# Chunks 16 to 31 of a chunked state-space attention: scores in four groups of 32 rows, scores and decay in the same four PSUM banks

## The chip, the core and the metric

The kernel runs on one core of a Trainium2 chip. The metric is the device time of one execution in microseconds, as the median of several runs. TensorE multiplies matrices into PSUM (eight banks of 512 fp32 values in each of 128 partitions), VectorE and ScalarE read PSUM and SBUF, GpSimd works on SBUF alone and issues DMAs, SyncE issues DMAs.

## The reference

Three layers follow one another: a chunked linear attention with decay (4 batches, 8 heads, 768 positions, head width 32, state width 16), a two-layer MoE with a leaky activation, and a gated two-layer MoE. Cut to what matters here:

```python
for c in range(nc):                         # chunks along the sequence
    cum = np.cumsum(la, axis=-1)
    L = np.exp(cum[:, :, :, None] - cum[:, :, None, :]) * causal
    CB = np.einsum('bhin,bhjn->bhij', Cc, Bc)
    y = np.einsum('bhij,bhjd->bhid', CB * L, xc)
    y += np.einsum('bhin,bhnd->bhid', Cc, state) * np.exp(cum)[..., None]
    state = decay_full * state + sum_j(Bc * xc * decay_from_j)
h = x @ w_in
x = (np.maximum(h, 0.0) + alpha * np.minimum(h, 0.0)) @ w_out
gate = 1.0 / (1.0 + np.exp(-(x @ w_gate)))
out = (gate * (x @ w_val)) @ w_out2
```

## The kernel before

The sequence is cut into chunks of T = 96 positions, eight for each batch, 32 in all. The state is carried as 16 further rows of the chunk, so W = 112 rows stand for 96 positions and 16 state entries. For one chunk c:

- `ev_decay(c)` multiplies a left tile `dl` with a right tile `dr` into the PSUM tile `d` (two banks, tag "d"), two matmuls of 384 columns, and ScalarE's exp turns that into `lt` (L337).
- `ev_scores(c)` computes C times B into the PSUM tile `cb` (two banks, tag "cb", L351). Each of its two matmuls uses 64 rows of the array: 4 heads of 16 state entries, with C laid out in blocks so that each head meets its own columns (4 x 96 = 384).
- `ev_weigh(c)` multiplies scores and decay on VectorE into `mt` (L358), and B with the last column of the decay into `bd` (L365; not in the last chunk of a batch).
- `ev_out(c)` runs `yd` = x times `mt` (L386), and x times `bd` for the next state (L380); ScalarE copies the state (L396) and the output (L398).

The first MoE layer is interleaved: from iteration `lead` = 7 on, each iteration i also does one step of it. `moe1_in` (L429) multiplies into the one-bank tile `h`, ScalarE makes `t` (L434), VectorE makes `g` from `h` and `t` (L436). In the next iteration `halves` splits `g` into `gh` (ScalarE, L449) and `gl` (VectorE, L450), and `moe1_out` (L473) accumulates into `acc`. When a run of such steps ends, `acc` is copied or added out (L485 to L488). Between them `feed(n, ...)` does n of the operations that unpack the MoE weights, on VectorE and ScalarE (L138 to L181); GpSimd fetches their raw words.

The schedule is manual: every engine does its instructions in the order in which the loop writes them. Iteration i writes, in turn: the product of scores and decay of chunk i, `halves` of the step before, the decay of chunk i + 1, some weight operations, the MoE step, the output of chunk i - 1, the scores of chunk i + 1, the MoE output of the step before, and more weight operations. Every tag in PSUM has one buffer here; a matmul into it waits until the readers of its last content are done. `load_cum`, `load_x` and `load_bc` issue the loads for chunk i + 3 on SyncE; B and C of four chunks (a group) come in five DMAs.

Of the kernel before, what the change touches and what calls it, by code (L numbers as in the profile page):

```python
# [18 lines left out]
T = 96  # L19
# [9 lines left out]
WG = 256  # L29

RAWS = 4

OPS = 7

# [13 lines left out]
def kernel(  # L48
# [46 lines left out]
    ring = ctx.enter_context(tc.tile_pool(name="ring", bufs=2))  # L95
    psum = ctx.enter_context(tc.tile_pool(name="psum", bufs=1, space=PSUM))
    dram = ctx.enter_context(tc.tile_pool(name="dram", bufs=1, space=DRAM))

    alpha_sb = cpool.tile([128, NF1], F32, name="alpha_sb")
    sign = cpool.tile([128, NF1], F32, name="sign")  # L100
# [117 lines left out]
    c0 = 4 * G * N + H  # L218
    misc = apool.tile([128, T + W], F32, name="misc")
    units_c = apool.tile([128, N], F32, name="units")  # L220
    mask_c = misc[0:T, 0:T]
    left_c = misc[0:T, T:T + W]
    eye_c = apool.tile([N, N], F32, name="eye")
# [26 lines left out]
    def load_x(c):  # L250
# [4 lines left out]
        if k == 0:  # L255
            nc.gpsimd.memset(t[T:W, 0:H * D], 0.0)

    def load_bc(c, e=None):


        if c < ND:
            BC[c] = aring.tile([128, W + 4 * T], F32, tag="bc0", name="bct", bufs=1)
            nc.sync.dma_start(out=BC[c], in_=bc0[:, c])
        else:
            g = c // G
            e = e or nc.sync
            e.dma_start(
                out=bt[g % NG][:, :, 0:T], in_=bc[g][:, 0].rearrange("p (g t) -> p g t", t=T)
            )
            src = bc[g][:, 1].rearrange("(m q) t -> q m t", q=NP)  # L270
# [39 lines left out]
            out=cum_d.rearrange("b h l s -> (b h l) s"), in_=bf(parts)  # L310
        )

    LT, MT, BD, CBT = {}, {}, {}, {}
    lead = -(-BL // T) + 1

    def ev_decay(c):

        d = psum.tile([W, 2, 512], F32, tag=("d", "acc")[c % 2] if c < lead else "d", name="d")
        for e in range(2):
            hs = slice(4 * e, 4 * e + 4)  # L320
            if c >= DIRECT:
                nc.tensor.matmul(  # L322
                    d[:, e, 0:4 * T], dl[c % NC], dr[c % NC][:, hs, :], start=True, stop=True
                )
                continue
            nc.tensor.matmul(
                d[:, e, 0:4 * T], early_l[:, c], early_r[:, hs, :],
                start=True, stop=False, skip_group_check=True,
            )
            for q in range(4):  # L330
                nc.tensor.matmul(
                    d[:, e, q * T:(q + 1) * T], early_i[:, 4 * e + q],
                    parts[0:2 * H, c * T:(c + 1) * T],
                    start=False, stop=True, skip_group_check=True,
                )
        LT[c] = t = aring.tile([W, H, T], F32, tag="lt", name="lt", bufs=2)
        nc.scalar.activation(  # L337
            t.rearrange("j (e h) t -> j e (h t)", e=2), d[:, :, 0:4 * T], AF.Exp
        )

    def ev_scores(c):

        cb = psum.tile([W, 2, 512], F32, tag="cb", name="cb")
        for e in range(2):
            r = slice(64 * e, 64 * e + 64)
            if c < ND:
                left, right = BC[c][r, 0:W], BC[c][r, W:]
            else:
                g, i = divmod(c, G)
                left, right = bt[g % NG][r, i], ct[g % NG][r, :, i * T:(i + 1) * T]  # L350
            nc.tensor.matmul(cb[:, e, 0:4 * T], left, right, start=True, stop=True)  # L351
        CBT[c] = cb

    def ev_weigh(c):
        MT[c] = m = aring.tile([W, H, T], F32, tag="mt", name="mt", bufs=2)

        split = "j (e q) t -> j e q t" if c < ND else "j (q e) t -> j e q t"
        nc.vector.tensor_tensor(  # L358
            m.rearrange(split, e=2),
            CBT.pop(c)[:, :, 0:4 * T].rearrange("j e (q t) -> j e q t", t=T),  # L360
            LT[c].rearrange(split, e=2), op=ALU.mult,
        )
        if c % CPB < CPB - 1:
            BD[c] = bd = aring.tile([W, H, N], F32, tag="bd", name="bd")
            nc.vector.tensor_tensor(  # L365
                bd, b_of(c), LT[c][:, :, T - 1:T].broadcast_to([W, H, N]), op=ALU.mult
            )

    def ev_out(c):

# [49 lines left out]
        nc.scalar.copy(t[:, 0], src)  # L420
        nc.vector.tensor_tensor(t[:, 1], src, bf(t[:, 0]), op=ALU.subtract)

    def moe1_in(k, f, tag):
        need(2 * (f // 2))
        h = psum.tile([128, BL], F32, tag=tag, name="h")
        w = win[f // 2][:, :, :, (f % 2) * 128:(f % 2 + 1) * 128]
        for i, (wl, xl) in enumerate(((1, 0), (0, 0), (0, 1))):
            for kt in range(KT):
                nc.tensor.matmul(  # L429
                    h, w[:, wl, kt, :], xh["m1", k][:, xl, kt, :],  # L430
                    start=(i == 0 and kt == 0), stop=(i == 2 and kt == KT - 1),
                )
        t = ring.tile([128, BL], F32, tag="s", name="t")
        nc.scalar.activation(t, h, AF.Identity, scale=sign[:, f:f + 1])  # L434
        g = ring.tile([128, BL], F32, tag="g", name="g")
        nc.vector.scalar_tensor_tensor(  # L436
            g, h, salpha[:, f:f + 1], t, op0=ALU.mult, op1=ALU.max
        )
        gt["m1", k, f] = g
# [23 lines left out]
    def moe1_out(k, f, two=True):  # L463
        need(2 * (f // 2) + 1)
        first, last = ends[k, f]
        if first:
            accs[0] += two
            acc[k] = psum.tile([128, KT, BL], F32, tag=("acc", "d")[accs[0] % 2], name="acc")
        gh, gl = gt.pop(("m1", k, f))
        w = wout[f // 2][:, :, f % 2, :]  # L470
        for i, (wl, g) in enumerate(((1, gh), (0, gh), (0, gl))):
            for m in range(KT):
                nc.tensor.matmul(  # L473
                    acc[k][:, m], w[:, wl, m * 128:(m + 1) * 128], g,
                    start=(first and i == 0), stop=(last and i == 2),
                )
        if last and two:
            moe1_done(k)
# [15 lines left out]
    def moe2_in(k, f, tag):  # L494
        need(first2 + 3 * (f // 2) + 1)
        gate = psum.tile([128, BL], F32, tag=tag, name="gate")
        if f % 2 == 0:
            vt[k] = psum.tile([128, 2, BL], F32, tag="cb", name="val")
# [15 lines left out]
    def moe2_out(k, f):  # L514
        need(first2 + 3 * (f // 2) + 2)
        if f == 0:
            po[k] = [psum.tile([128, 2, 512], F32, tag=t, name="po") for t in ("acc", "d")]
        o = po[k]
        ph, pl = gt.pop(("m2", k, f))
        w = w2["out", f // 2][:, :, f % 2, :]  # L520
# [138 lines left out]
    def moe2_pair(k, j, before):  # L659
# [6 lines left out]
        a = two(psum.tile([128, BL], F32, tag="h", name="pa"))  # L666
        b = two(psum.tile([128, BL], F32, tag="y", name="pb"))
        if j % 2 == 0:
            vt[k] = psum.tile([128, 2, BL], F32, tag="cb", name="pc")
# [75 lines left out]
    with tc.manual_schedule():  # L745
# [5 lines left out]
        def step_in(i, tag):  # L751
            kind, k, f = steps[i]
            (moe1_in if kind == "m1" else moe2_in)(k, f, tag)

        def step_out(i, **kw):
            kind, k, f = steps[i]
# [13 lines left out]
        def keep_busy(n):  # L770
            p = psum.tile([128, 512], F32, tag="h", name="nobody")
            for _ in range(n):
                nc.tensor.matmul(p, heat[:, 0:128], heat, start=True, stop=True)
# [31 lines left out]
            load_x(i)  # L805
        take_up()
        nc.gpsimd.dma_start(out=alpha_sb, in_=alpha)

        def setup_units(j):
            nc.gpsimd.tensor_scalar(  # L810
                bt[j][:, :, T:W], units_c.unsqueeze(1).broadcast_to([128, G, N]),
                2.0, None, op0=ALU.mult,
            )

        copy_eye(0)
        setup_units(0)
# [88 lines left out]
        at = 0  # L905
        for i in range(NCH + 1):
            go = i >= lead
            if i < NCH:
                ev_weigh(i)

            if i == lead // 2 + 1:
# [5 lines left out]
            if i == 1:  # L917
                setup_left(1)
                load_cum(4)
                scale(0)  # L920
                for j in range(2):
                    setup_right(j)
                keep_busy(2)
            if 1 <= i <= 3:
                follow(i)
                ahead[0] += i != 2
                take_up()
# [7 lines left out]
                halves(steps[at - 1])  # L935
            if at > 1 and ends[steps[at - 2][1:]][1]:
                moe1_done(steps[at - 2][1])
            if i + 1 < NCH:
                ev_decay(i + 1)
            now = 0 if i == 0 else EARLY if not go else FIRST if at < half else LATER  # L940
            feed(now // 2, first2)
            if go:
                step_in(at, "h")
            if i > 0:
                ev_out(i - 1)
            if i + 1 < NCH:
                ev_scores(i + 1)
            if not go:
                keep_busy(3 if i < 3 else 2)
# [9 lines left out]
            if i == -(-2 * BL // T):  # L959
                split_x("m1", 1)  # L960
        need(first2 - 1)
        actx.close()
        p2 = ctx.enter_context(tc.tile_pool(name="p2", bufs=1))

# [127 lines left out]
```

## Time and profile before

| | |
|---|---|
| median of 3 runs | 636.93 us (636.29 to 638.09) |
| the profiled execution's own time | 638.78 us |
| its span in the profile | 637.0 us |
| TensorE busy | 625.9 us, 98% of the span |
| VectorE busy | 520.4 us, 82% |
| ScalarE busy | 364.7 us, 57% |
| GpSimd busy | 39.4 us, 6% |
| chunks 16 to 31, from the decay of 16 to the end of the last step | 71.5 to 147.2 us |

The span runs from the first to the last instruction of the profile. The execution's own time is longer by what lies around it. A busy share is a mean over all stages.

### The profile page before, as it was taken

To read this page: it belongs to the slowest core of one execution; us is meant where nothing else is said; L and a number is where in the kernel's file an instruction comes from. 1 tells how busy PE (TensorE), PEld (TensorE's weight loads), DVE (VectorE), ACT (ScalarE), POOL (GpSimd) and SP (SyncE) were. 2 spreads that over 40 slices of the span, in tenths; PEclk is the share of its full clock that TensorE was granted. 3 is DMA by queue.
4 is the path that set the end of the run, shared out by engine and by line. 5 is a ranking of instruction groups with operands and counts; after the bars stand their busy time and mean duration, and the time that the engine had idled before them with its cause. 6 is when DMAs were issued, how large, how long until landed. Compare 5 with 4: busy or idle time off the path is not lost.

```text
span 637.0 us, 11146 instructions
## 1 busy us (share of the span) xinstructions
PE 625.9 (98%) x4336; PEld 519.1 (81%) x4336; DVE 520.4 (82%) x910; ACT 364.7 (57%) x729; POOL 39.4 (6%) x68
## 2 busy tenths in 40 slices
PE   8799999999999999999999999999999999999997
PEld 4356666667888888888888888999999999999996
DVE  7799988865888878777676988888888888888876
ACT  7788877865666666566555435534534534534443
POOL 9211001000000000000000000000000000000000
PEclk9899999999999999999999999999999999999999
DMA  6744334410221221220000000100100100100100
GB/s 189 223 143 157 113 117 123 132 44 2 67 66 34 66 67 34 66 66 1 1 1 1 1 1 1 34 1 2 34 1 1 35 1 2 34 1 2 34 1 33
DMA packets 19270, 30.69 MB, mean 48 GB/s; under 512 B 7330, under 2 KB 14658, under 8 KB 19218
## 3 DMA queue, kind: packets, MB, share of 16 engines
q0 software_dynamic: 5232, 18.44, 9.2%
q1 hardware_dynamic: 13474, 11.08, 6.1%
q8 instruction: 34, 0.56, 0.4%
q10 hardware_dynamic: 512, 0.47, 0.2%
q14 instruction: 18, 0.15, 0.1%
HBM read 26.57 MB, written 3.34 MB: 47 GB/s over the span
## 4 chain that ended last, share of the span: by engine, by line
PE 92%; ACT 3%; DVE 2%; DMA 1%; issue 1%; POOL 0%; ACTq 0%; DVEq 0%
PE acc L473 21%; PE h L429 20%; PE pb L610 10%; PE po L552 10%; PE pa L610 7%; PE pc L610 7%; PE po L557 5%; PE cb L351 3%; PE gate L504 3%; PE val L504 3%; PE yd L386 1%; PE d L322 1%; DMA raw<-in_moe_w_in_dram 1%; PE yd L380 1%; ACT lt L337 1%
## 5 line engine op out<-in xcount | busy, mean ns | idle before, releaser
L429 PE MATMUL h<-xh,win 128*128 128x512 f32 x576 | 146.9, 390 | 0.5 <-ACT xh L420 0.5
L429 PEld LDWEIGHTS h<-xh,win 128*128 128x128 f32 x576 | 107.7, 188 | 22.3 <-ACT xh L420 0.8
L473 PE MATMUL acc<-gh,wout 128*128 128x512 f32 x384 | 105.8, 397 | 0.6 <-ACT x L398 0.6
L436 DVE SCALAR_TENSOR_TENSOR g<-h,salpha,t 128x512 f32<-128x512 f32 x96 | 71.9, 749 | 41.5 <-ACT t L434 41.2
L473 PEld LDWEIGHTS acc<-gh,wout 128*128 128x128 f32 x384 | 70.1, 188 | 27.0 <-ACT t L434 10.6
L434 ACT ACTIVATE t<-h,sign 128x512 f32<-128x512 f32 x96 | 66.0, 688 | 43.7 <-PE h L429 43.2
L449 ACT CAST gh<-g 128x512 fp32r<-128x512 f32 x96 | 59.7, 621 | 43.0 <-DVE g L436 43.0
L450 DVE TENSOR_TENSOR gl<-g,gh 128x512 fp32r<-128x512 f32 x96 | 66.0, 688 | 15.9 <-ACT gh L449 14.8
L719 ACT ACTIVATE s<-cs 128x512 f32<-128x512 f32 x30 | 19.0, 633 | 92.5 <-DVE cs L718 92.5
L552 PE MATMUL po<-w2out,gh 128*128 128x512 f32 x240 | 65.3, 394 | 0.0
L450 DVE TENSOR_TENSOR gl<-p,gh 128x512 fp32r<-128x512 f32 (+1 forms) x74 | 49.7, 672 | 12.6 <-ACT gh L449 12.6
L473 PE MATMUL acc<-gl,wout 128*128 128x512 f32 x192 | 59.2, 389 | 0.0
L449 ACT CAST gh<-p 128x512 fp32r<-128x512 f32 (+1 forms) x74 | 45.0, 610 | 20.8 <-DVE p L725 12.0
L552 PEld LDWEIGHTS po<-w2out,gh 128*128 128x128 f32 x240 | 41.8, 189 | 6.1
L610 PE MATMUL pa<-xh,w2in 128*128 128x256 f32 x300 | 44.0, 282 | 0.0
L473 PEld LDWEIGHTS acc<-gl,wout 128*128 128x128 f32 x192 | 36.0, 188 | 7.8
L557 PEld LDWEIGHTS po<-w2out,gl 128*128 128x128 f32 x240 | 36.3, 188 | 5.5 <-DVE gl L450 0.9
L610 PEld LDWEIGHTS pa<-xh,w2in 128*128 128x128 f32 x300 | 39.3, 190 | 0.0
L557 PE MATMUL po<-w2out,gl 128*128 128x256 f32 x240 | 38.0, 280 | 0.0
L337 ACT ACTIVATE lt<-d 112x768 f32<-112x768 f32 x32 | 26.0, 812 | 13.2 <-PE d L322 12.2
L694 DVE TENSOR_TENSOR cs<-pb,cs 128x512 f32<-128x512 f32 x30 | 20.7, 689 | 14.3 <-PE pb L610 14.3
L358 DVE TENSOR_TENSOR mt<-cb,lt 112x768 f32<-112x768 f32 x32 | 30.4, 949 | 0.2 <-ACT lt L337 0.2
(165 smaller groups left out, 1040.1 us busy)
## 6 DMA issues: line engine op xcount, KB each, us to landing
raw<-in_moe_w_out_dram POOLq DMA_DIRECT2D x14, 512.0 KB, 4.1
xs<-in_xb_dram SPq DMA_DIRECT2D x32, 144.0 KB
raw<-in_moe_w_in_dram POOLq DMA_DIRECT2D x8, 512.0 KB, 4.3
raw<-in_moe_w_gate_dram POOLq DMA_DIRECT2D x6, 512.0 KB, 4.1
raw<-in_moe_w_val_dram POOLq DMA_DIRECT2D x6, 512.0 KB, 4.1
out_dram<-osb SPq DMA_DIRECT2D x10, 256.0 KB
bt<-in_bc_dram SPq DMA_DIRECT2D x7, 192.0 KB
ct<-in_bc_dram SPq DMA_DIRECT2D x28, 48.0 KB
```

Source lines behind the costliest of these rows:

```text
L337: nc.scalar.activation(t.rearrange("j (e h) t -> j e (h t)", e=2), d[:, :, 0:4 * T], AF.Exp)
L358: nc.vector.tensor_tensor(m.rearrange(split, e=2), CBT.pop(c)[:, :, 0:4 * T].rearrange("j e (q t) -> j e q t", t=T), LT[c].rearrange(split ...
L429: nc.tensor.matmul(h, w[:, wl, kt, :], xh["m1", k][:, xl, kt, :], start=(i == 0 and kt == 0), stop=(i == 2 and kt == KT - 1),)
L434: nc.scalar.activation(t, h, AF.Identity, scale=sign[:, f:f + 1])
L436: nc.vector.scalar_tensor_tensor(g, h, salpha[:, f:f + 1], t, op0=ALU.mult, op1=ALU.max)
L449: nc.scalar.copy(gh[:, cs], g[:, cs])
L450: nc.vector.tensor_tensor(gl[:, cs], g[:, cs], bf(gh[:, cs]), op=ALU.subtract)
L473: nc.tensor.matmul(acc[k][:, m], w[:, wl, m * 128:(m + 1) * 128], g, start=(first and i == 0), stop=(last and i == 2),)
L504: nc.tensor.matmul(p, w[:, wl, kt, :], xh["m2", k][:, xl, kt, :], start=(i == 0 and kt == 0), stop=(i == 2 and kt == KT - 1),)
L552: nc.tensor.matmul(o[e][:, u].rearrange("p (l d) -> p l d", l=2), ph[:, ts], w, start=(f == 0), stop=False, skip_group_check=True,)
L557: nc.tensor.matmul(o[e][:, u, 0:DM], pl[:, ts], w[:, 0, :], start=False, stop=last, skip_group_check=True,)
L610: nc.tensor.matmul(bank[:, e], left_of(e, j, a, wl), right_of(k, b, xl), start=first and e == i == 0, stop=i == 2, skip_group_check=True,)
```

## The change

It applies to chunks 16 (`ZC`) to 31.

- Scores: four matmuls of 32 rows (2 heads) and 192 columns, in place of two of 64 rows and 384. B and C are loaded in another order of partitions for that: ten DMAs for a group of four chunks in place of five. GpSimd zeroes the C tiles and sets the unit columns once for each of the two buffers.
- Decay: four matmuls of 192 columns. Scores and decay of a chunk stand in one PSUM tile `four` of four banks, in each bank 192 columns of scores and then 192 of decay. It lies in a PSUM pool of the attention's own (`px`), which is closed and opened again where the tiles "cb" and "d" give way to "four" and after the last chunk.
- Order: the scores of chunk i + 1 stand ahead of the output of chunk i - 1, and their product with the decay is written in the same iteration, between `t` and `g` of the MoE step, in place of at the start of the next.
- `bd` is computed on GpSimd, after the VectorE instruction that stands ahead of `mt`.
- The weight operations are 3 or 4 in an iteration (4 in every third), in place of 4.

```diff
+    def open_banks():
+        if px:
+            px[0].close()
+        px[:] = [ExitStack()]
+        px.append(px[0].enter_context(tc.tile_pool(name="px", bufs=1, space=PSUM)))
+    def banks(tag, name):
+        pool = px[1] if tag in ("cb", "d") else psum
+        return pool.tile([128, 2, 512], F32, tag=tag, name=name)
...
     def load_bc(c, e=None):
+            if g >= ZG:
+                t = bt[g % NG], ct[g % NG][:, 0:2]
+                if g < ZG + NG:
+                    setup_units(g % NG, units_z)
+                    nc.gpsimd.memset(t[1], 0.0)
+                for h in range(2):
+                    src = bc[g][64 * h:64 * h + 64].rearrange("(n k) w t -> w k n t", k=NP)
+                    for i in range(G):
+                        e.dma_start(
+                            out=t[0][h:128:2, i, 0:T], in_=src[0][:, :, i * T:(i + 1) * T]
+                        )
+                    e.dma_start(out=t[1][h:128:2, h, :], in_=src[1])
+                return
...
     def ev_decay(c):
+        if c >= ZC:
+            four[c] = px[1].tile([W, 4, 512], F32, tag="four", name="four")
+            d = four[c][:, :, 2 * T:4 * T]
+            for q in range(4):
+                nc.tensor.matmul(
+                    d[:, q], dl[c % NC], dr[c % NC][:, 2 * q:2 * q + 2, :], start=True, stop=True,
+                )
+            nc.scalar.activation(t.rearrange("j (q e) t -> j q (e t)", e=2), d, AF.Exp)
+            return
...
     def ev_scores(c):
+        if c >= ZC:
+            g, i = divmod(c, G)
+            CBT[c] = cb = four.pop(c)[:, :, 0:2 * T]
+            for q in range(4):
+                r = slice(32 * q, 32 * q + 32)
+                nc.tensor.matmul(
+                    cb[:, q], bt[g % NG][r, i], ct[g % NG][r, 0:2, i * T:(i + 1) * T],
+                    start=True, stop=True,
+                )
+            return
...
     def ev_weigh(c):
+            if c >= ZC:
+                behind(nc.gpsimd.tensor_tensor(*args, op=ALU.mult), last)
+            else:
+                nc.vector.tensor_tensor(*args, op=ALU.mult)
...
-    def moe1_in(k, f, tag):
+    def moe1_in(k, f, tag, later=None):
         nc.scalar.activation(t, h, AF.Identity, scale=sign[:, f:f + 1])
+        if later:
+            later()
         g = ring.tile([128, BL], F32, tag="g", name="g")
...
-            if i < NCH:
+            if i < min(NCH, ZC):
                 ev_weigh(i)
...
+            if i + 1 in (ZC, NCH + 1):
+                open_banks()
             if i + 1 < NCH:
                 ev_decay(i + 1)
             now = 0 if i == 0 else EARLY if not go else FIRST if at < half else LATER
+            if i + 1 >= ZC:
+                now = 4 if at % 3 == 0 else 3
             feed(now // 2, first2)
+            def chunk():
+                if i + 1 < NCH:
+                    ev_scores(i + 1)
+                ev_out(i - 1)
+                if i + 1 < NCH:
+                    ev_weigh(i + 1)
             if go:
-                step_in(at, "h")
-            if i > 0:
-                ev_out(i - 1)
-            if i + 1 < NCH:
+                step_in(at, "h", later=chunk if i + 1 >= ZC else None)
+            if i + 1 < ZC:
+                if i > 0:
+                    ev_out(i - 1)
                 ev_scores(i + 1)
```

TensorE's row in iteration 17 before, from the decay of chunk 18 to the MoE output (the names after "waits" are the semaphores of the engines, and of SyncE's DMAs where they begin with DMAHW):

```order
L322 MATMUL d<-dr_107,dl_104 112x384 [waits DMAHW2_49,DMAHW1_49,Activation_49]
L322 MATMUL d<-dr_107,dl_104 112x384
L429 MATMUL h<-xh,win_74 128x512 [waits DVE_49]
L429 MATMUL h<-xh,win_74 128x512 x5
L380 MATMUL yd<-xs_102,bd 16x32 [waits DMAHW0_49,Activation_49,Pool_49]
L380 MATMUL yd<-xs_102,bd 16x32 x7
L386 MATMUL yd<-mt,xs_102 32x96 x8
L351 MATMUL cb<-ct_112,bt_110 112x384 [waits DVE_49]
L351 MATMUL cb<-ct_112,bt_110 112x384
L473 MATMUL acc<-gh,wout_78 128x512 [waits Activation_49]
L473 MATMUL acc<-gh,wout_78 128x512 x3
L473 MATMUL acc<-gl,wout_78 128x512 [waits DVE_49]
```

The same iteration after the change:

```order
L362 MATMUL four<-dr_111,dl_108 112x192 [waits DMAHW7_49,DMAHW6_49,DVE_49]
L362 MATMUL four<-dr_111,dl_108 112x192 x3
L509 MATMUL h<-xh,win_77 128x512 [waits DVE_49]
L509 MATMUL h<-xh,win_77 128x512 x5
L396 MATMUL four<-ct_116,bt_114 112x192 [waits DMAHW0_49,Activation_49]
L396 MATMUL four<-ct_116,bt_114 112x192 x3
L457 MATMUL yd<-xs_106,bd 16x32 [waits PE_49,Pool_49]
L457 MATMUL yd<-xs_106,bd 16x32 x7
L463 MATMUL yd<-mt,xs_106 32x96 x8
L555 MATMUL acc<-gh,wout_81 128x512 x4
L555 MATMUL acc<-gl,wout_81 128x512 [waits DVE_49]
L555 MATMUL acc<-gl,wout_81 128x512
```

The scores (L351 before, L396 after) stand ahead of the output rows, not behind them. They waited for VectorE and now wait for ScalarE; the decay (L322 before, L362 after) waited for ScalarE and now waits for VectorE.

VectorE's row in iteration 17 before, from the product `mt` of chunk 17 to the weight operations behind `g`:

```order
L358 TENSOR_TENSOR mt<-cb,lt 112x2x4x96 [waits PE_49]
L365 TENSOR_TENSOR bd<-xs_103,lt 112x128 [waits DMAHW0_49]
L450 TENSOR_TENSOR gl<-g,gh 128x512 [waits Activation_49]
L172 TENSOR_SCALAR mag<-mag 128x512
L436 SCALAR_TENSOR_TENSOR g<-h,salpha,t 128x512 [waits Activation_49]
L155 TENSOR_TENSOR wout_80<-mag,wout_80 128x512
L176 SCALAR_TENSOR_TENSOR raw<-raw 128x512 [waits DVE_49]
```

The same iteration after the change, up to the weight operation behind `g`:

```order
L532 TENSOR_TENSOR gl<-g,gh 128x512 [waits Activation_49]
L182 TENSOR_SCALAR raw<-raw 128x512 [waits DMASW5_49]
L430 TENSOR_TENSOR mt<-four,lt 112x768 [waits PE_49,Activation_49]
L518 SCALAR_TENSOR_TENSOR g<-h,salpha,t 128x512 [waits Activation_49]
L190 TENSOR_SCALAR mag<-mag 128x512
```

Now `mt` is that of chunk 18, and it stands directly ahead of `g` rather than ahead of `gl`; it waits for ScalarE besides TensorE; `bd` is gone from the row, and two weight operations stand here in place of three.

## Rows read from the trace of the kernel before

**Rows 1.** The page: busy time, share of the span and instructions of two engines.

```profile
PE 625.9 (98%) x4336; PEld 519.1 (81%) x4336; DVE 520.4 (82%) x910; ACT 364.7 (57%) x729; POOL 39.4 (6%) x68
```

**Rows 2.** Windows: busy us and records by engine, granted clock, from 71.5 to 147.2 us.

```profile
core 0: us, PE busy (x) PEld busy (x) DVE busy (x) ACT busy (x) POOL busy (x), PEclk, DMA share, GB/s
71.50:147.20 75.70, 75.70 (x770) 51.44 (x769) 60.86 (x108) 57.71 (x138) 6.09 (x9) 1.00 0.34 100
```

**Rows 3.** The chain by time in one chunk: start us, us, what.

```profile
104.67 0.35 PE d L322 x2
105.02 1.40 PE h L429 x6
106.42 0.24 PE yd L380 x16
106.66 0.33 PE yd L386 x16
106.99 0.83 PE cb L351 x4
107.82 1.58 PE acc L473 x6
```

**Rows 4.** Timeline of TensorE: start us, us, engine, line, operation, count of records.

```profile
106.92 0.58 PE L351 MATMUL cb<-ct,bt 64*112 64x384 f32 x2
```

**Rows 5.** Timeline, first decay of the kernel, narrow matmuls and their weight loads.

```profile
7.43 0.46 PEld L331 LDWEIGHTS d<-parts,wout 16*112 16x112 f32 x4 [0.19 <-issue]
7.44 0.59 PE L331 MATMUL d<-parts,wout 16*112 16x96 f32 x4
```

**Rows 6.** Groups by line and shape, whole span: busy us, mean ns of one.

```profile
L434 ACT ACTIVATE t<-h,sign 128x512 f32<-128x512 f32 x96 | 66.0, 688 | 43.7 <-PE h L429 43.2
...
L358 DVE TENSOR_TENSOR mt<-cb,lt 112x768 f32<-112x768 f32 x32 | 30.4, 949 | 0.2 <-ACT lt L337 0.2
...
L337 ACT ACTIVATE lt<-d 112x768 f32<-112x768 f32 x32 | 26.0, 812 | 13.2 <-PE d L322 12.2 <-POOL xs L790 0.5 <-POOL scrap L872 0.5
...
L396 ACT COPY xs<-yd 16x64 f32<-16x64 f32 x112 | 22.7, 203 | 1.7
...
L365 DVE TENSOR_TENSOR bd<-xs,lt 112x128 f32<-112x128 f32 x28 | 7.8, 280 | 0.0
...
L153 ACT CAST win<-mag 128x512 fp32r<-128x512 f32 x10 | 6.2, 616 | 0.0
```

**Rows 7.** Timeline from the decay of chunk 16 on.

```profile
71.42 0.95 DVE L358 TENSOR_TENSOR mt<-cb,lt 112x768 f32<-112x768 f32 x1
71.49 0.51 PE L322 MATMUL d<-dr,dl 114*112 114x384 f32 x2
...
72.03 0.30 SPq L285 DMA_DIRECT2D dl<-cum_d  x1
72.04 0.81 ACT L337 ACTIVATE lt<-d 112x768 f32<-112x768 f32 x1 [0.37 <-PE d L322]
...
76.42 0.59 ACT L487 COPY x<-acc 128x512 f32<-128x512 f32 x1 [0.58 <-PE acc L473]
```

**Rows 8.** Timeline of a later chunk, VectorE and ScalarE.

```profile
107.17 0.75 DVE L436 SCALAR_TENSOR_TENSOR g<-h,salpha,t 128x512 f32<-128x512 f32 x1 [1.14 <-ACT t L434]
...
107.84 0.42 DVE L172 TENSOR_SCALAR mag<-mag 128x512 f32<-128x512 f32 x1
108.02 0.32 ACT L398 COPY x<-yd 128x192 f32<-128x192 f32 x1
...
108.24 0.62 ACT L449 CAST gh<-g 128x512 fp32r<-128x512 f32 x1
```

**Rows 9.** Groups of GpSimd by line and shape.

```profile
L790 POOL COPY xs<-eye 16x128 f32<-16x128 f32 x6 | 2.1, 382 | 0.1
...
L810 POOL TENSOR_SCALAR bt<-units 128x64 f32<-128x64 f32 x2 | 0.9, 448 | 0.6 <-DMA units<-in_k_misc_dram 0.5
```

More of the change, by code (lines that the diff above doesn't have):

```diff
@@ L31 @@
 RAWS = 4
+ZG = 4
 OPS = 7
@@ L97 @@
     dram = ctx.enter_context(tc.tile_pool(name="dram", bufs=1, space=DRAM))
+    px = []
+    def open_banks():
[7 more added lines that the diff above has]
+        return pool.tile([128, 2, 512], F32, tag=tag, name=name)
     alpha_sb = cpool.tile([128, NF1], F32, name="alpha_sb")
@@ L220 @@
     units_c = apool.tile([128, N], F32, name="units")
+    units_z = apool.tile([128, N], F32, name="units_z")
+    ZC = ZG * G
     mask_c = misc[0:T, 0:T]
@@ L256, in load_x, with setup_units @@
             nc.gpsimd.memset(t[T:W, 0:H * D], 0.0)
+    def setup_units(j, units=units_c):
+        nc.gpsimd.tensor_scalar(
+            bt[j][:, :, T:W], units.unsqueeze(1).broadcast_to([128, G, N]),
+            2.0, None, op0=ALU.mult,
+        )
     def load_bc(c, e=None):
@@ L311, in store_cum @@
         )
-    LT, MT, BD, CBT = {}, {}, {}, {}
+    LT, MT, BD, CBT, four = {}, {}, {}, {}, {}
     lead = -(-BL // T) + 1
     def ev_decay(c):
-        d = psum.tile([W, 2, 512], F32, tag=("d", "acc")[c % 2] if c < lead else "d", name="d")
+        LT[c] = t = aring.tile([W, H, T], F32, tag="lt", name="lt", bufs=2)
+        if c >= ZC:
[7 more added lines that the diff above has]
+            return
+        d = banks(("d", "acc")[c % 2] if c < lead else "d", "d")[0:W]
         for e in range(2):
@@ L335, in ev_decay @@
                 )
-        LT[c] = t = aring.tile([W, H, T], F32, tag="lt", name="lt", bufs=2)
         nc.scalar.activation(
@@ L341, in ev_scores @@
     def ev_scores(c):
-        cb = psum.tile([W, 2, 512], F32, tag="cb", name="cb")
+        if c >= ZC:
[6 more added lines that the diff above has]
+                    start=True, stop=True,
+                )
+            return
+        cb = banks("cb", "cb")[0:W]
         for e in range(2):
@@ L352, in ev_scores, with ahead_of_this, behind @@
         CBT[c] = cb
+    def ahead_of_this(e):
+        of = e.engine
+        return next(i for i in reversed(nc.cur_bb.bb.instructions) if i.engine == of)
+    def behind(ins, last):
+        tc.add_manual_dep(
+            ins.ins, last.name,
+            mybir.DependencyInfo(mybir.DependencyClass.Sync, mybir.DependencyReason.DATA),
+            reason="order",
+        )
     def ev_weigh(c):
         MT[c] = m = aring.tile([W, H, T], F32, tag="mt", name="mt", bufs=2)
[L357 to L362, printed above, removed]
+        last = ahead_of_this(nc.vector)
+        if c >= ZC:
+            split = lambda t: t.rearrange("j (q e) t -> j q (e t)", e=2)
+            nc.vector.tensor_tensor(split(m), CBT.pop(c), split(LT[c]), op=ALU.mult)
+        else:
+            split = "j (e q) t -> j e q t" if c < ND else "j (q e) t -> j e q t"
+            nc.vector.tensor_tensor(
+                m.rearrange(split, e=2),
+                CBT.pop(c)[:, :, 0:4 * T].rearrange("j e (q t) -> j e q t", t=T),
+                LT[c].rearrange(split, e=2), op=ALU.mult,
+            )
         if c % CPB < CPB - 1:
             BD[c] = bd = aring.tile([W, H, N], F32, tag="bd", name="bd")
-            nc.vector.tensor_tensor(
-                bd, b_of(c), LT[c][:, :, T - 1:T].broadcast_to([W, H, N]), op=ALU.mult
-            )
+            args = (bd, b_of(c), LT[c][:, :, T - 1:T].broadcast_to([W, H, N]))
+            if c >= ZC:
+                behind(nc.gpsimd.tensor_tensor(*args, op=ALU.mult), last)
+            else:
+                nc.vector.tensor_tensor(*args, op=ALU.mult)
     def ev_out(c):
@@ L421, in split_x @@
         nc.vector.tensor_tensor(t[:, 1], src, bf(t[:, 0]), op=ALU.subtract)
-    def moe1_in(k, f, tag):
+    def moe1_in(k, f, tag, later=None):
         need(2 * (f // 2))
-        h = psum.tile([128, BL], F32, tag=tag, name="h")
+        if tag == "cb":
+            h = banks(tag, "h")[:, 0]
+        else:
+            h = psum.tile([128, BL], F32, tag=tag, name="h")
         w = win[f // 2][:, :, :, (f % 2) * 128:(f % 2 + 1) * 128]
@@ L467, in moe1_out @@
             accs[0] += two
-            acc[k] = psum.tile([128, KT, BL], F32, tag=("acc", "d")[accs[0] % 2], name="acc")
+            acc[k] = banks(("acc", "d")[accs[0] % 2], "acc")
         gh, gl = gt.pop(("m1", k, f))
@@ L497, in moe2_in @@
         if f % 2 == 0:
-            vt[k] = psum.tile([128, 2, BL], F32, tag="cb", name="val")
+            vt[k] = banks("cb", "val")
         val = vt[k][:, f % 2]
@@ L516, in moe2_out @@
         if f == 0:
-            po[k] = [psum.tile([128, 2, 512], F32, tag=t, name="po") for t in ("acc", "d")]
+            po[k] = [banks(t, "po") for t in ("acc", "d")]
         o = po[k]
@@ L668, in moe2_pair @@
         if j % 2 == 0:
-            vt[k] = psum.tile([128, 2, BL], F32, tag="cb", name="pc")
+            vt[k] = banks("cb", "pc")
         c = two(vt[k][:, j % 2])
@@ L749, with step_in @@
         last1 = steps.index(("m1", NBK - 1, 0))
-        def step_in(i, tag):
+        def step_in(i, tag, **kw):
             kind, k, f = steps[i]
-            (moe1_in if kind == "m1" else moe2_in)(k, f, tag)
+            (moe1_in if kind == "m1" else moe2_in)(k, f, tag, **kw)
         def step_out(i, **kw):
@@ L807 @@
         nc.gpsimd.dma_start(out=alpha_sb, in_=alpha)
[L809 to L813, printed above, removed]
         copy_eye(0)
@@ L923 @@
                 keep_busy(2)
+            if i == lead:
+                for h in range(2):
+                    nc.gpsimd.dma_start(
+                        out=units_z[h:128:2],
+                        in_=k_misc[64 * h:64 * h + 64, 0:N].rearrange("(n k) c -> k n c", k=NP),
+                    )
             if 1 <= i <= 3:
@@ L937 @@
                 moe1_done(steps[at - 2][1])
+            if i + 1 in (ZC, NCH + 1):
+                open_banks()
             if i + 1 < NCH:
@@ L961 @@
         need(first2 - 1)
+        ctx.callback(px[0].close)
         actx.close()
```

## The prediction

> **What bounds it now.** I read the page's busy times first: TensorE is busy for 98% of the span, VectorE for 82% [rows 1]. That is a mean over stages, so the second view is the stretch in which chunks 16 to 31 run, from the decay of chunk 16 at 71.5 us to the end of the last chunk's step at 147.2 us. There TensorE is busy for all 75.70 us, VectorE for 60.86 and ScalarE for 57.71, at a granted clock of 1.00, the upper of its two levels, 2.4 GHz [rows 2]. Third, the chain of work through one chunk: it goes from TensorE to TensorE with no other engine between, decay 0.35, MoE step 1.40, attention output 0.24 + 0.33, scores 0.83, MoE output 1.58 us [rows 3]: 4.73 us a chunk. So here TensorE's own work sets the time. A microsecond taken from VectorE is worth nothing, one taken from TensorE is worth one, as long as no wait appears.
>
> **Scores: -0.33 us a chunk.** A score matmul stands in the trace as two records, one after the other on the same columns, and two row groups run side by side: the first two records of 384 columns, about 0.57 us each with their drain, fit in 0.58 us [rows 4]. What does a column cost? The attention output's 16 records of 96 columns, four side by side, take 0.33 us [rows 3], so 0.083 for 96 columns, 0.86 ns a column. By that a score record of 384 columns streams for 0.33, the two in turn 0.66, and the remaining 0.17 of the 0.83 is weight load and the change of array layout. After the change there are four row groups with 192 columns each. If all four run side by side the stream is 2 x 192 x 0.86 ns = 0.33, and with the same 0.17 the scores cost 0.50. Bounds: 0.46, if the smaller loads hide a little, and 0.83, if only two groups ever run together, since four then cost two times two. No row shows four row groups at once; the rows show two row groups (the scores) and four column groups (the output) without loss, so I take 0.50, and keep 0.83 as a rival.
>
> Here a rule speaks against the change. The Trainium skill, TensorE: Matmul & The Clock Gate, section Measured speedup vs the span model, gives 3.07 times, not 4, for four row tiles of 32. No run here shows it yet; an estimate by that page is 4 x 0.33 / 3.07 = 0.43 of streaming, so scores of 0.60. I don't put that in the sum, but incomplete overlap is a rival below.
>
> **Decay: +0.07 us a chunk.** Two matmuls of 384 columns become four of 192 with the same weights. Before, the two take 0.35 [rows 3], 0.175 each. Narrow matmuls of this kind are in the trace once, in the early chunks, at 96 columns: four in 0.59 us, the last with its own 0.26, so (0.59 - 0.26) / 3 = 0.11 apart, and their four weight loads, 0.46 in all with 0.17 for the last, (0.46 - 0.17) / 3 = 0.10 apart [rows 5]. 192 columns stream for half of 0.175, 0.09; so the load of 112 columns sets the pace, and four cost about 0.42. Bounds: 0.35, if nothing is lost, and 0.48. Narrow matmuls at a quarter of the rate would take 0.35 each, as 384 columns take 0.175; the 0.11 for 96 columns is under the 0.175 of that rate, though with 16 rows and not 114, so I leave it 2 in 100.
>
> The chunk then costs 4.73 - 0.33 + 0.07 = 4.47 us. Output and MoE steps keep their work, and three changes of layout stay three, in another order. Sixteen chunks: 16 x 0.26 = **-4.2 us**.
>
> **The new waits.** Scores and decay now share four banks with one buffer. So the scores of a chunk wait for ScalarE's exp to have read its decay, and the next decay waits for VectorE's product mt. I follow one chunk from its decay at 0, with the durations of [rows 6, 8], 0.20 us from a TensorE end to the reader (0.35 of decay from 71.49, exp at 72.04 [rows 7]), an overlap of successive instructions of 0.08 on VectorE (g ends 107.92, the next starts 107.84) and 0.10 on ScalarE (a copy ends 108.34, gh starts 108.24) [rows 8].
> - Decay ends 0.42, the MoE step 1.82, scores 2.32, output 2.89, MoE output 4.47.
> - exp runs 0.62 to 1.43. The scores are due at 1.82: 0.39 to spare.
> - mt runs 2.52 to 3.47, and the next decay is due at 4.47: 1.0 to spare. g, now behind mt, runs 3.39 to 4.14; the next MoE step, which overwrites what it reads, is due at 4.89.
> - ScalarE: t to 2.71; the state copies 3.09 to 3.94 and x to 4.26; in about half of the chunks a weight operation of 0.62 from 4.16 to 4.78; gh from 4.68 to 5.30, which is 0.83 in the next chunk; exp then 0.73 to 1.54. The scores still have 0.28 to spare.
> - In the two chunks where a finished half of an accumulation is copied out (L487, 0.59 us ahead of exp [rows 7], and the same eight chunks later), exp ends at 2.03 and the scores wait about 0.25: **+0.5 us** for both. Before, that copy cost TensorE nothing.
> - Once, the decay of chunk 16 has to wait until the old banks are free, so for mt of chunk 15. That runs from 71.42 for 0.95, while the decay started at 71.49 [rows 7]: 72.41 - 71.49 = **+0.9 us**, bounds 0.5 and 1.3.
>
> **At no price.** bd leaves VectorE for GpSimd: 28 in the kernel at 0.28 us [rows 6], 14 of them in these chunks. VectorE is not the bound, so nothing is won. On GpSimd the nearest rows are a copy of 128 elements at 0.38 and a scale of 64 at 0.45 us [rows 9]; between 0.4 and 1.5 us it is hidden, since its reader comes a whole chunk later. What could be late behind it is exp two chunks on, which overwrites its input; it starts too early for that. The weight operations at 3.33 rather than 4 a chunk still end in the loop. The ten smaller loads per group of four chunks, in place of five, are issued on SyncE two to three chunks ahead; at the 0.3 us apiece of SyncE's issues in [rows 7] that is 3 us of 18, hidden. Were a group's load a whole chunk late, that would be 4.5 us four times; I see nothing that takes this cover away.
>
> **Sum.** -4.2 + 0.5 + 0.9 = -2.8 us. The profiled execution took 638.78 us (span 637.0, 1.8 around it), so it would take 636.0. The median of the runs is 636.93, and the same 2.8 us give **634.1**.
>
> **Rivals.**
> - *The forecast*, 634.1, with a range of its own from 632.7 (decay 0.35, scores 0.50) to 635.3 (decay 0.48, waits twice as long). Chance 0.60.
> - *The four groups overlap, but not fully.* Streaming between 0.33 and 0.66, halfway 0.50: scores 0.67, a gain of 0.09 x 16 = 1.4, eaten by the waits' 1.4: 636.9, within 0.3%. For it: no row shows four banks written at once. Against: two groups lose nothing. By the 3.07 of the Trainium skill, TensorE: Matmul & The Clock Gate, an estimate is 635.7. Chance 0.13.
> - *Only two groups run at a time*, because weight loads or bank writes allow no more, so the change doesn't do what it says. Scores stay at 0.83, decay costs 0.07: 16 x 0.07 + 1.4 = +2.5 us, 639.4, slower. It comes out slower by over 0.3% from scores of 0.79 on. The same evidence for and against; chance 0.09.
> - *The scores wait for exp in every chunk.* For it: exp stands behind gh, which stands behind g, which now stands behind mt, and mt behind the scores: that ring takes 0.50 + 0.20 + 0.87 + 0.75 + 0.05 + 0.52 + 0.81 + 0.05 = 3.75 us, and by way of the copies with a weight operation 4.2, against 4.47. Against: it closes with 0.3 to spare. Each 0.1 us beyond costs 1.6; at 0.15 it is +2.4, 636.5, no change; from 0.3 on it ends slower. Chance 0.13.
> - *Narrow decay at a quarter rate*: four at 0.35 add 1.05 a chunk, 16.8 in place of 1.1, about 650. Chance 0.02. The last 0.03 stay with what I don't see.
>
> **Range and chances.** A measurement of this kernel can tell about 0.3% (1.9 us) from no change, so faster means under 635.0. Of the forecast's 0.60 some 0.50 lie under that, and 0.05 come from milder cases of the overlap and waiting rivals: faster 0.55. Same: 0.10 + 0.10 + 0.09 = 0.29. Slower: 0.09 + 0.02 + 0.03 and a little from the waits, 0.16. A range from 632.6 to 637.6 holds the forecast, the partial overlap and most of the waits, and leaves out two at a time and the quarter rate: about 8 in 10.
>
> **What would show it.** In the profile after: a chunk of 4.47 us on the chain; score records starting four together, with the second four 0.17 us behind; decay of four at about 0.10 apart; a single wait of TensorE for mt near 72 us; two waits of the scores for ScalarE, each after an accumulator copy. Wrong would be: score records in pairs, scores waiting for exp throughout, or TensorE idle after the output for another reason.

## The result, and the profile after

| | before | after |
|---|---|---|
| median | 637.12 us (636.29 to 638.09, 6 runs) | 640.59 us (639.22 to 642.55, 6 runs) |
| ratio, 95% interval | | 1.006 (1.0039 to 1.0081) |
| profiled execution, span | 638.78, 637.0 us | 640.40, 638.5 us |

The change makes the kernel 3.5 us, 0.6%, slower. The forecast was 634.1 us with a range up to 637.6; the time lies outside the range.

The page of the kernel after, the busy line that answers to [rows 1], and two of the groups by line, each with the idle time of its engine just ahead and what ended it:

```profile
PE 624.7 (98%) x4432; PEld 521.8 (82%) x4432; DVE 518.0 (81%) x896; ACT 364.0 (57%) x729; POOL 48.2 (8%) x88
...
L555 PE MATMUL acc<-gh,wout 128*128 128x512 f32 x384 | 105.8, 397 | 3.2 <-DVE wout L173 2.7
...
L430 DVE TENSOR_TENSOR mt<-four,lt 112x768 f32<-112x768 f32 x16 | 15.3, 957 | 15.7 <-PE yd L463 15.7
```

TensorE is busy for 1.2 us less and still ends later. Two entries are new. The MoE output (L555) waited 2.7 us for one weight operation on VectorE. And VectorE idles about 1 us on average ahead of the 16 products `mt`, and what ends that idle time is the attention output `yd`, not the scores.

Windows of the kernel after (busy us and records by engine, granted clock, DMA share, GB/s), one of the same length as in [rows 2], and one after the loop's long wait:

```profile
69.60:145.30 75.70, 71.95 (x858) 52.31 (x858) 57.39 (x94) 57.18 (x137) 12.89 (x25) 1.00 0.34 100
...
146.50:150.00 3.50, 3.50 (x29) 2.31 (x31) 0.00 (x0) 0.10 (x1) 0.00 (x0) 0.51 0.00 0
```

Before, TensorE was busy in all of the 75.70 us. Now it idles 3.75 of them, and in the second window, behind the longest of its waits, it works at a granted clock of 0.51, the lower level.

The chain by time of the kernel after (start, us, what): first one regular chunk, the answer to [rows 3], then a chunk whose scores wait for exp, then the end of the loop:

```profile
88.33 0.39 PE four L362 x4
88.71 1.50 PE h L509 x6
90.21 0.53 PE four L396 x8
90.74 0.24 PE yd L457 x16
90.97 0.33 PE yd L463 x16
91.31 1.59 PE acc L555 x6
...
112.22 0.58 ACT x L569
112.80 0.72 ACT lt L365
...
113.57 0.59 PE four L396 x8
...
133.96 0.66 DVE g L518
134.62 0.61 DVE win L173
...
135.27 1.65 PE h L509 x6
...
142.24 0.38 PE yd L463 x16
...
142.71 0.96 DVE mt L430
143.67 0.66 DVE g L518
144.33 0.33 DVE mag L190
144.66 0.61 DVE wout L173
...
145.32 1.93 PE acc L555 x6
147.25 2.57 PE h L509 x6
```

The scores take 0.53 in place of 0.83 and the decay 0.39 in place of 0.35, close to the forecast's 0.50 and 0.42. But the MoE step `h` takes 1.50 (1.49 in most chunks) in place of 1.40, so a regular chunk takes 4.56 us and not 4.47. At the end of the loop TensorE finishes `yd` and then has nothing to do until VectorE has made `mt`, `g` and two operations of the weights: 2.74 us of idle. The MoE output and step after it take 1.93 and 2.57 where 1.58 and 1.38 are usual.

The timeline of the kernel after (start, us, engine, line, operation, count; in brackets the idle time of the engine ahead and what ended it): the first decay of the new kind, and one regular chunk:

```profile
67.41 0.68 DVE L194 SCALAR_TENSOR_TENSOR raw<-raw 128x512 uint32<-128x512 uint32 x1
68.13 0.69 DVE L199 SCALAR_TENSOR_TENSOR mag<-mag,raw 128x512 uint32<-128x512 uint32 x1
68.74 0.95 DVE L433 TENSOR_TENSOR mt<-cb,lt 112x768 f32<-112x768 f32 x1
69.79 0.61 PE L362 MATMUL four<-dr,dl 114*112 114x192 f32 x4 [0.81 <-ACT gh L531]
...
86.59 0.41 POOL L442 TENSOR_TENSOR bd<-xs,lt 112x128 f32<-112x128 f32 x1 [4.03 <-PE yd L457]
...
86.88 0.96 DVE L430 TENSOR_TENSOR mt<-four,lt 112x768 f32<-112x768 f32 x1 [0.96 <-PE yd L463]
...
87.75 0.74 DVE L518 SCALAR_TENSOR_TENSOR g<-h,salpha,t 128x512 f32<-128x512 f32 x1
...
88.17 0.55 PE L362 MATMUL four<-dr,dl 114*112 114x192 f32 x4
...
88.55 1.22 PEld L509 LDWEIGHTS h<-xh,win 128*128 128x128 f32 x6
88.55 1.66 PE L509 MATMUL h<-xh,win 128*128 128x512 f32 x6
...
90.14 0.43 PE L396 MATMUL four<-ct,bt 32*112 32x192 f32 x4
```

Four score records start together, at 90.14, where [rows 4] had two. The decay at 69.79 shows how a wait is read: the row names ScalarE's `gh`, but `gh` had ended at 69.00 (it started at 68.48 for 0.52 on the chain). What ended at 69.69 is `mt` of chunk 15, behind two weight operations on VectorE.

**Where the 3.5 us come from.** I add up the intervals from decay to decay of the two profiled executions (before, after), from the decay of chunk 15 on, at 66.78 and 64.09. The profiled execution of before had lost 2.7 us ahead of that, in a part that the change hardly touches (its granted clock over the first 40 us was 0.96, that of after 1.00), so the two profiled executions differ by less than what the table adds up.

| stretch | before | after | difference |
|---|---|---|---|
| decay 15 to 16 | 4.71 | 5.70 | +0.99 |
| 15 intervals, 16 to 31, were they all regular | 70.76 | 15 x 4.56 = 68.40 | -2.36 |
| two chunks with scores that wait for exp (4.73, 4.72) | | | +0.33 |
| two more, around one late `mt` (4.66, 4.83) | | | +0.37 |
| decay 30 to 31 (5.14): the step waits for a weight | | | +0.58 |
| decay 31 to the MoE output behind the loop's last wait | 10.86 | 14.94 | +4.08 |
| from decay 15 to there | 86.33 | 90.29 | +3.96 |

Behind that point they take 483.9 and 484.1 us to the end of the span. The late `mt` starts at 105.49, 0.5 us after the output ahead of it, with VectorE idle; what holds it there stays open.

### The profile page after: what moved, and what is told of

Same layout as the page of the kernel before. It is cut to its first block, busy times and chain, and to the rows that moved or that the text cites. A ratio compares the mean times of both kernels' runs of the same rounds, so it can differ in the third digit from the quotient of the medians.

```text
span 638.5 us, 11411 instructions
## 1 busy us (share of the span) xinstructions
PE 624.7 (98%) x4432; PEld 521.8 (82%) x4432; DVE 518.0 (81%) x896; ACT 364.0 (57%) x729; POOL 48.2 (8%) x88
## 4 chain that ended last, share of the span: by engine, by line
PE 89%; DVE 5%; ACT 3%; issue 1%; DMA 1%; DVEq 0%; ACTq 0%
PE h L509 20%; PE acc L555 20%; PE pb L692 10%; PE po L634 10%; PE pa L692 7%; PE pc L692 7%; PE po L639 5%; PE gate L586 3%; PE val L586 3%; PE four L396 1%; PE yd L463 1%; PE four L362 1%; PE cb L409 1%; PE nobody L855 1%; DVE g L518 1%
## 5 line engine op out<-in xcount | busy, mean ns | idle before, releaser
L509 PE MATMUL h<-xh,win 128*128 128x512 f32 x576 | 149.6, 396 | 0.8 <-DVE win L173 0.4
L555 PE MATMUL acc<-gh,wout 128*128 128x512 f32 x384 | 105.8, 397 | 3.2 <-DVE wout L173 2.7
L555 PEld LDWEIGHTS acc<-gh,wout 128*128 128x128 f32 x384 | 70.2, 188 | 23.1 <-ACT t L514 3.5
L555 PE MATMUL acc<-gl,wout 128*128 128x512 f32 x192 | 59.6, 392 | 0.0
L555 PEld LDWEIGHTS acc<-gl,wout 128*128 128x128 f32 x192 | 36.1, 188 | 7.8
L430 DVE TENSOR_TENSOR mt<-four,lt 112x768 f32<-112x768 f32 x16 | 15.3, 957 | 15.7 <-PE yd L463 15.7
L473 ACT COPY xs<-yd 16x64 f32<-16x64 f32 x112 | 22.6, 202 | 6.7 <-PE yd L463 5.4
```

The costliest lines, as they stand in the source:

```text
L473: nc.scalar.copy(state[:, :, e], ds[32 * e:32 * e + N])
L509: nc.tensor.matmul(h, w[:, wl, kt, :], xh["m1", k][:, xl, kt, :], start=(i == 0 and kt == 0), stop=(i == 2 and kt == KT - 1),)
L555: nc.tensor.matmul(acc[k][:, m], w[:, wl, m * 128:(m + 1) * 128], g, start=(first and i == 0), stop=(last and i == 2),)
```

## The experiments

The theory after the result: the weight operations, paced at 3 or 4 an iteration, are late at the end of the loop, and that costs about 4 us (pacing). The rival: the new ring of waits through the four shared banks holds TensorE back, and more weight operations on VectorE would make that worse (ring). Besides, the 0.09 us that each MoE step had grown by had to be explained: by the narrow decay ahead of it, or by `g`. Intervals are 95%; the ratio is always to the kernel before, run on the same chip (median 637.0 for the first four, 636.68 for the rest).

**e1_feed4.** The kernel after with the old pacing.

```diff
-                now = 4 if at % 3 == 0 else 3
+                now = LATER
```

> The changed kernel with four weight operations in every iteration again, in place of three or four. Theory A (pacing): the changed kernel lost its gain where the last MoE steps of the loop wait for weights that are unpacked too late: 0.6 us ahead of the step of chunk 30, 2.8 us ahead of an MoE output in the next iteration, and 1.3 us in the step behind that at half the granted clock. All three go: 640.6 - 4.7 = 635.9 us, 0.2% under before. Theory B (ring): the loss comes from scores and decay in the same four banks, each waiting for the other's reader; more weight operations between make that worse: 640 us or more, and TensorE's waits for exp and mt in the trace.

Measured: 636.61 us, 0.9994 (0.9983 to 1.0005), 4.0 us under the kernel after. In the windows of this kernel TensorE's idle time shrinks from 3.75 to 1.38 us, though VectorE has more to do:

```profile
69.60:145.30 75.70, 74.32 (x869) 53.77 (x867) 59.25 (x95) 57.60 (x138) 13.69 (x25) 1.00 0.34 100
```

So the pacing cost these 4 us, and the ring did not. More weight operations are not free either: in this trace one `mt` (79.69) stands directly behind a weight operation, the next MoE step has to wait for `g` behind it, and that chunk takes 4.85 us, 0.29 more than the regular 4.56. What remains is a change that wins almost nothing. By the decays of this trace, the 2.4 us of the regular chunks are given back in part by the once-only wait (0.99), by chunks that are late (0.57 together) and behind the decay of chunk 31 (0.32), where a step waits for `g` once more.

**e2_before_slowfeed.** The same pacing put alone into the kernel before.

```diff
+            if i + 1 >= 16:
+                now = 4 if at % 3 == 0 else 3
```

> The kernel before, with only the pacing of the change: three or four weight operations an iteration from the decay of chunk 16 on. Theory A: the same weights come late here too. They stand behind g alone, not behind mt and g, so the MoE output waits about 1.2 us rather than 2.8, and the clock holds: 637.1 + 1.2 = 638.3 us. Theory B: pacing costs nothing, 637.1 us.

Measured: 638.50 us, 1.0026 (1.0015 to 1.0037). The late weights cost here too, but less. Timeline of this kernel, TensorE, at the end of the loop:

```profile
142.59 0.90 PE L351 MATMUL cb<-ct,bt 64*112 64x384 f32 x4
144.73 1.17 PE L473 MATMUL acc<-gh,wout 128*128 128x512 f32 x4 [1.25 <-DVE wout L155]
```

The wait for the same operation is 1.25 and not 2.74, and the MoE output and step behind it take 1.62 and 1.38, close to the usual. Two things lie between: the scores (L351) stand behind `yd` here and fill 0.83 us, and VectorE goes to the weights after `g` without a `mt` that waits for `yd`. With the order of the change the same lateness costs more than twice as much (4.0 us between e1 and the kernel after, 1.5 here). How much of that each of the two makes was not measured apart.

**e3_before_narrow.** The kernel before with the decay of chunks 16 on as four matmuls of 192 columns, into its old two banks.

```diff
-                nc.tensor.matmul(
-                    d[:, e, 0:4 * T], dl[c % NC], dr[c % NC][:, hs, :], start=True, stop=True
-                )
+                for p in range(2 if c >= 16 else 1):
+                    w = 2 if c >= 16 else 4
+                    nc.tensor.matmul(
+                        d[:, e, p * w * T:(p + 1) * w * T], dl[c % NC],
+                        dr[c % NC][:, 4 * e + p * w:4 * e + (p + 1) * w, :],
+                        start=True, stop=True,
+                    )
```

> The kernel before with each decay of chunks 16 to 31 as four matmuls of 192 columns into the same two banks, and nothing else. The prediction's price of 0.07 us a chunk gives +1.1: 638.2 us. The trace of the changed kernel shows 0.39 for the four and an MoE step whose first weight load is no longer hidden, 0.14 us a chunk together: +2.2, 639.3 us. If narrow matmuls cost nothing: 637.1 us.

Measured: 637.64 us, 1.0006 (0.9994 to 1.0017). The chain of this kernel:

```profile
103.57 0.39 PE d L324 x4
103.96 1.40 PE h L433 x6
```

The narrow decay costs 0.04 (0.39 for 0.35) and leaves the step behind it at 1.40. So the longer step of the kernel after does not come from the decay; I had thought so before this run, and that was wrong.

**e4_feed4_mt3.** e1 with a third buffer for `mt`.

```diff
-        MT[c] = m = aring.tile([W, H, T], F32, tag="mt", name="mt", bufs=2)
+        MT[c] = m = aring.tile([W, H, T], F32, tag="mt", name="mt", bufs=3)
```

> The changed kernel with four weight operations an iteration and a third buffer for mt. In the trace mt starts when the output's matmuls end, not when the scores end, since it overwrites what the output of two chunks before reads. With a third buffer mt, g, gh and exp come 0.57 us earlier in each chunk, and the two waits of the scores for exp (0.26 us each) go: 0.5 us under the kernel with four weight operations, so 635.4 us. If mt's place does not matter: the same time as that one, 635.9 us.

Measured: 634.30 us, 0.9955 (0.994 to 0.9969), 2.3 us under e1 and more than I expected. Timeline of this kernel, one regular chunk:

```profile
86.44 0.96 DVE L430 TENSOR_TENSOR mt<-four,lt 112x768 f32<-112x768 f32 x1 [0.45 <-PE four L396]
...
87.31 0.74 DVE L518 SCALAR_TENSOR_TENSOR g<-h,salpha,t 128x512 f32<-128x512 f32 x1
...
88.30 0.55 PE L362 MATMUL four<-dr,dl 114*112 114x192 f32 x4
...
88.59 1.23 PEld L509 LDWEIGHTS h<-xh,win 128*128 128x128 f32 x6
88.68 1.57 PE L509 MATMUL h<-xh,win 128*128 128x512 f32 x6
```

`mt` is now released by the scores and starts 2.61 us after its decay (83.83 to 86.44) in place of 3.28, 0.67 earlier. `g` ends at 88.05, long before the step, whose first weight load starts 0.29 us after the decay (0.38 in the kernel after, 88.17 to 88.55) and runs ahead of the first matmul again. The step is back to 1.41 and the chunk to 4.47 or 4.48, the forecast's number. So the 0.09 was `g`.

**e5_early15.** e4, and `mt` of chunk 15 written right after its scores instead of at the start of the next iteration.

```diff
-            if i < min(NCH, ZC):
+            if i < min(NCH, ZC - 1):
                 ev_weigh(i)
...
                 ev_scores(i + 1)
+                if i + 1 == ZC - 1:
+                    ev_weigh(i + 1)
```

> Four weight operations, three buffers for mt, and the product mt of chunk 15 written right behind its scores, before the MoE output, so that the old banks are free when the decay of chunk 16 comes. If the 5.70 us from the decay of chunk 15 to that of chunk 16 (4.71 before) are the wait for that product, 0.97 us go: 634.3 - 1.0 = 633.3 us. If closing and opening the PSUM pool costs the time by itself, it stays at 634.3.

Measured: 633.10 us, 0.9947 (0.9935 to 0.9959), the fastest version here, by the ratio 0.5% or 3.4 us under the kernel before. The chain of this kernel where the banks change hands:

```profile
67.81 1.59 PE acc L555 x6
69.40 0.39 PE four L362 x4
69.78 1.40 PE h L509 x6
```

The decay of chunk 16 follows the MoE output without a gap, 4.72 us after that of chunk 15 in place of 5.70. The trace shows this 1.0 us; the times alone would not, since the ratios of e4 and e5 lie 0.5 us apart and their intervals overlap. Closing and opening the pool stays in this kernel and costs nothing that the chain shows.

**e6_mt3.** The kernel after with the third buffer alone (the edit of e4), at its own pacing.

> The changed kernel with three buffers for mt and its own pacing of three or four weight operations. If pacing and buffer act apart: 640.6 less the 2.3 us that the third buffer gave beside four operations, less up to 0.6 as the late weight operations then start 0.57 us earlier behind mt and g: 637.8 us, and the MoE output still waits about 2.2 us for its weights. If the third buffer alone cures the changed kernel: 634.5 us.

Measured: 637.13 us, 1.0014 (1.0002 to 1.0026): by the ratios 0.46%, 2.9 us better than the kernel after. The chain of this kernel at the end of the loop:

```profile
140.16 0.57 PE four L396 x8
...
140.83 0.96 DVE mt L430
141.78 0.66 DVE g L518
142.44 0.33 DVE mag L190
142.78 0.61 DVE wout L173
...
143.43 2.93 PE acc L555 x6
```

and the window over it (columns as above), which shows the lower clock again:

```profile
143.00:146.50 3.50, 3.07 (x7) 2.51 (x8) 0.98 (x2) 0.10 (x1) 0.00 (x0) 0.51 0.00 0
```

`mt` starts right after the scores, so the weights come 0.65 us sooner behind it, but they are still late: TensorE idles for 2.17 us up to 143.43 and then needs 2.93 in place of 1.58. Buffer and pacing are separate faults, and each is worth repairing alone (2.9 us here, 4.0 in e1).

**e7_bd_dve.** e4 with `bd` back on VectorE.

```diff
-            if c >= ZC:
-                behind(nc.gpsimd.tensor_tensor(*args, op=ALU.mult), last)
-            else:
-                nc.vector.tensor_tensor(*args, op=ALU.mult)
+            nc.vector.tensor_tensor(*args, op=ALU.mult)
```

> Four weight operations, three buffers for mt, and bd on VectorE again, right behind mt and ahead of g. If VectorE has room, as the prediction said, no change: 634.3 us. If the 0.28 us of bd ahead of g bring the wait of the MoE step for g back (0.1 us in 14 chunks): 635.5 us.

Measured: 634.76 us, 0.9971 (0.9961 to 0.9981); e4's interval ends at 0.9969, so the two overlap. Regular chunks are 4.48 us in both. Whether GpSimd is worth up to 1 us, through single late chunks (one of 5.02 us in this trace), stays open.

**e8_catch_up.** The kernel after with 3 or 4 operations up to step 12, and 5 from step 13 on.

```diff
-                now = 4 if at % 3 == 0 else 3
+                now = 5 if at >= 13 else 4 if at % 3 == 0 else 3
```

> The changed kernel, two buffers for mt, with its own pacing of three or four weight operations up to chunk 20 and five an iteration from there on, so that the weights are all unpacked by the iteration in which four an iteration would have them. If only the lateness at the end costs: as with four throughout, 636.6 us. If fewer operations per chunk cost by themselves, or more of them beside the four banks: 639 us or more.

Measured: 636.42 us, 1.0001 (0.9991 to 1.0012), the same as e1 within the intervals. So fewer operations earlier in the loop show neither a gain nor a loss here, and the 4 us go with the lateness at its end. Five operations in an iteration have a price too: one chunk of this trace takes 5.14 us, as its exp stands on ScalarE behind two weight operations, `gh` and the copy of an accumulator, and the scores wait 0.6 us for it.

## Why the prediction was wrong

**The step that failed: "The weight operations at 3.33 rather than 4 a chunk still end in the loop."** I priced this at nothing and named no work that hides it. Ending in the loop is not the point: each MoE step and each MoE output needs its own weights by its own place in the loop, and the function `need` writes whatever operations are still missing directly ahead of it. Counted from the program, the step of iteration 29 needs 110 operations and the last outputs in the loop need 117. At 4 an iteration all of these are done by iteration 28. At 3 or 4 the 110th is only written at the very end of iteration 28, behind `mt` and `g`, so the step finds it unfinished; and there are 114 after iteration 29 and 115 in the middle of 30, where the output needs 117. The missing two (`mag` L190 and `wout` L173) are then written on VectorE at that very place: behind `mt` and `g`. The price is in the table above: 0.58 for the step that waits for `win`, 2.74 for the output that waits for `wout`, and 0.35 + 1.19 = 1.54 because the output and step after the wait ran partly at the lower clock (0.51 in the window from 146.5 on), 4.9 us in all. e1 gets back 4.0 of them by the pacing alone, and e2 shows the same fault in the kernel before.

**The second: "mt runs 2.52 to 3.47".** The walk through one chunk released `mt` by the scores. But `mt` has two buffers, and the output of chunk i - 1, which the new order puts between the scores of chunk i + 1 and `mt` of chunk i + 1, still reads the buffer that this `mt` is to overwrite. So it waits for the end of the output: it starts 3.28 us after its decay (83.60 to 86.88). `g` behind it ends at 4.89, where the walk had the next step due at 4.89 and `g` done at 4.14. All of the 0.75 us of slack was gone, and the first weight load of each step from chunk 17 on is no longer hidden: 0.09 x 15 = 1.35 us. e4 shows it, since one buffer more brings the chunk to 4.48. The program could have told: `mt` has two buffers there, so its writer waits for the reader of two chunks ago, and the new order had put that reader ahead of it.

Both steps and the late `mt` make up the miss: 4.86 + 1.35 + 0.37 = 6.6 us, where 640.59 lies 6.5 above 634.1, and where the table's +3.96 lies 6.8 above the forecast's -2.8. The cause of the late `mt` is open.

One sum of the prediction does not come out either. The forecast's own range, 632.7 to 635.3, should by the conditions that stand beside it be 633.0 (decay 0.35) to 636.5 (decay 0.48 and waits twice as long). That made "faster" look likelier than the terms allowed, but it is not the cause of the miss.

**What was right.**
- Scores: 0.53 us for a forecast of 0.50. All four row groups run together; the second four records start about 0.25 us behind the first, where 0.17 was forecast. The Trainium skill, TensorE: Matmul & The Clock Gate, section Measured speedup vs the span model, with its 3.07 times for four row tiles, had given an estimate of 0.60; the trace lies nearer to the full overlap.
- Decay: 0.39 us for 0.42, and no quarter rate. With the scores at 0.53 that rival falls, and so do those of partial overlap (0.67) and of two groups (0.83).
- The once-only wait of the decay of chunk 16: +0.99 for +0.9. Its cause is the forecast's, `mt` of chunk 15; e5 removes it.
- The waits of scores for exp: two, each behind the copy of an accumulator (`x` L569, then `lt`, then `four` L396 in the chain); each makes its chunk 0.17 longer, where 0.25 was forecast. In the other chunks the scores follow the MoE step without a gap, so the rival in which they wait for exp in every chunk falls too.
- `bd` on GpSimd: 0.41 us, hidden. The ten loads: no wait of TensorE for them in the loop.
- The regular chunk of 4.47 us exists, in e4 and e5. The gain asked of the change was there and was given back by the two conditions named above and the once-only wait.
- One of the named signs of being wrong is what came: TensorE idle after the output for another reason.

The rival that ended slower (two groups at a time, 639.4) came near the time by another mechanism; it is refuted by the score records.

## What to carry to other kernels

When work that feeds a later stage is paced slower, don't ask whether it all gets done, but count at each consumer how many operations must be done by then and how many are. Here the last consumers decided, and what was forced there landed behind whatever stood on that engine. When an instruction is moved past another, look at who read the buffer that it writes: with two buffers, a writer that is moved behind the reader of two rounds ago must wait for that reader, and a listing of the order does not show this by itself. A slack worked out on paper is worth no more than the latest release that goes into it.

## What the runs showed of the hardware

- Four groups of 32 rows, with 192 columns each into four banks, run together: in the kernel after four records start within 0.02 us of one another (from 90.14 on), and eight take 0.53 us on the chain, where four records of two 64-row groups with 384 columns took 0.83.
- An idle stretch of TensorE can cost twice, once by itself and once in the steps behind it. In the kernel after, the granted clock behind an idle stretch of 2.74 us was 1.00 up to 146.3 us and 0.50 from 147.3 to 149.8. In e6, behind one of 2.17 us, it was 0.51 in the window from 143.0 to 146.5 shown above. In e2, behind one of 1.25 us, it stayed at 1.00. Windows of the kernel after, then one of e2:

```profile
145.30:146.30 1.00, 0.98 (x4) 0.84 (x5) 0.56 (x1) 0.00 (x0) 0.00 (x0) 1.00 0.00 0
...
147.30:148.30 1.00, 1.00 (x3) 0.74 (x3) 0.00 (x0) 0.00 (x0) 0.00 (x0) 0.50 0.00 0
148.30:149.80 1.50, 1.50 (x11) 0.73 (x12) 0.00 (x0) 0.00 (x0) 0.00 (x0) 0.50 0.00 0
...
144.50:148.00 3.50, 3.27 (x40) 2.51 (x44) 1.55 (x3) 0.26 (x2) 0.00 (x0) 1.00 0.02 5
```

- When the first weight load of six matmuls is held until just before them, it is no longer hidden. In the kernel after, load and first matmul of the MoE step start together (88.55), and the step takes 1.49 us; in e4 the load starts 0.09 us ahead (88.59, 88.68), and the step takes 1.41.
